# elu+1 split between VectorE and GpSimd, one task for the memory products, and another seed for the planned order

## The chip, the cores and the metric

The kernel runs on one core of a Trainium2 chip. Its metric is device time in microseconds, the median of several runs. The engines in the profile are PE (TensorE, matrix multiplications; PEld is its weight load), DVE (VectorE), ACT (ScalarE), POOL (GpSimd) and SP (SyncE, which here issues DMAs). Each engine works through its own list of instructions in order and waits on semaphores for what other engines have to deliver.

## The reference

The input `x` has 2048 tokens of 512 features in bfloat16. Two branches are mixed by a gate per token: a gated attention with a compressive memory over four segments of 512 tokens and 32 heads of width 16, and a gated feed-forward layer of width 1792.

```python
phi = lambda t: jnp.where(t > 0, t + 1.0, jnp.exp(t))
for s in range(N):                       # four segments of 512 tokens
    logits = einsum('bhqd,bhkd->bhqk', qs, ks) * scale + mask
    a_dot = einsum('bhqk,bhkd->bhqd', softmax(logits), vs)
    pq = phi(qs)
    num = einsum('bhld,bhde->bhle', pq, M)
    den = einsum('bhld,bhd->bhl', pq, z)[..., None] + 1e-06
    outs.append(g * (num / den) + (1.0 - g) * a_dot)
    pk = phi(ks)
    M = M + einsum('bhld,bhle->bhde', pk, vs)
    z = z + einsum('bhld->bhd', pk)
a = concat(outs) @ wo
b = (gelu(x @ w_gate) * (x @ w_up)) @ w_down
out = sigmoid(x . gate_w) * a + (1 - sigmoid(x . gate_w)) * b
```

## The kernel before

**Layout.** `x` is held transposed (`xT`, features on the partitions) and the weights lie in on-chip memory. Everything on PE runs in tiles of 128 partitions by 512 tokens, accumulated in PSUM, of which there are eight banks (`ps`). In the attention phase most matrix products are split into four narrow ones that run side by side (`dense`, L479); one such quad works 512 columns.

**Stages.** In the first 66 us the keys, queries and values of segment 0 and the gate projections of all segments are computed (L565, L475), and ScalarE applies gelu. Then comes the attention phase. Each segment has 20 logit slots (`logit_slot`, L735): each fills two pairs of PSUM banks, ScalarE takes the exponential into `pT` (L757, two instructions of 128x1024 a slot) and GpSimd masks the diagonal blocks (L766). After some slots come the products with the values (`pv_group`, L785), which VectorE transposes out of PSUM (L803) and normalizes (L813 to L829).

**Fillers.** Between the slots PE computes other things: the up projections (`up_group`, L479 with `wup`, taken out of PSUM by VectorE in L657), the queries, keys and values of the next segment (`qk_group`, `v_group`, taken out by L314 or L316), the update of the memory (`m_update`, L894), the memory's denominator and numerator for the present segment (`mem_den` with `zbd`, `mem_num` with `Mbd`) and the output of the previous segment (`out_group`). `NUPS` says how many up groups go with each segment.

**elu+1.** `phi` makes a map of keys or queries for two chunks of 128 features at once, a tile of 128x1024. ScalarE writes the exponential to `E` (L847); VectorE writes max(x, 0) + 1 to `Q` (L852) and then the minimum of `E` and `Q` to the map (L856), since elu+1 is min(exp(x), max(x, 0) + 1). It is run twelve times: for the keys of segments 0, 1 and 2 (two each, `phi_k`) and the queries of segments 1, 2 and 3 (two each, `phi_q`). A key map goes through two DMA transposes on the sync queue (L883) and is the stationary operand of the memory update. A query map is read by the denominator and numerator products. There is one buffer each for `E`, `Q` and `pkT`.

**Memory.** After the second update of a segment VectorE forms `Mbd` from the accumulated memory in four products (L918) on 32 partitions each, and `zbd` (L922). In the planner the four are four tasks.

**The order.** It is not written out by hand. `Sched` takes all tasks with an engine, a cost in nanoseconds, dependencies, buffers taken and freed, and a priority, and simulates the engines once, on the host. At each step the engine that can start soonest takes, among the tasks that are ready, the one of smallest priority. Logit slots are held to a pace (`due`), which spreads the remaining dense work of PE over the remaining slots. Tasks marked `port=True` are ones that the planner lets wait for a GpSimd task that is running, and the other way round. The priorities of fillers on PE get a random offset, drawn with `SEED` between -`SPREAD` and +`SPREAD`. The instructions are emitted in the resulting order, and on the chip every engine keeps to it.

Of the kernel before, what the change touches and what calls it, by code (L numbers as in the profile page):

```python
# [10 lines left out]
ALU = mybir.AluOpType  # L11
# [6 lines left out]
DH = 16  # L18
# [16 lines left out]
SLACK = 300  # L35
PORTPEN = 0
NWARM = 6
NUPS = (28, 10, 9, 9)
ATT = 5
SEED = 1  # L40
SPREAD = 1.5
SHAPES = {"gen": [(b,) for b in range(NBANK)],
          "pair": [(b, b + 1) for b in range(NBANK - 1)]}
WIDTH = {k: len(v[0]) for k, v in SHAPES.items()}
# [14 lines left out]
class Sched:  # L59
# [10 lines left out]
    def __init__(self, rings):  # L70
        self.tasks = []
        self.bufs = rings
        self.rng = Random(SEED)

    def add(self, engs, cost, fn, **kw):

        if "PE" in engs and 0 < kw["prio"] < 9000:
            kw["prio"] += self.rng.uniform(-SPREAD, SPREAD)
        engs = {engs: cost} if isinstance(engs, str) else dict(zip(engs, cost))
        t = Task(engs, fn, **kw)  # L80
        t.seq = len(self.tasks)
        self.tasks.append(t)
        return t
# [205 lines left out]
def kernel(  # L289
# [15 lines left out]
    nc = tc.nc  # L305
# [20 lines left out]
    add = S.add  # L326

    def ctile(name, shape, dtype=BF):
        return cp.tile(shape, dtype, name=name, tag=name)
# [16 lines left out]
    def rtile(ring, shape, dtype=BF, pool=None):  # L346
        pool = pool or (pools["wp"] if ring in WP else rp)
        return pool.tile(shape, dtype, name=ring, tag=ring, bufs=RINGS[ring])
# [16 lines left out]
    zbd = ctile("zbd", [P, NCH * (P + 2)])  # L365
    bdeb = ctile("bdeb", [P, NCH, 8, DH])
    Mbd = ctile("Mbd", [P, NCH, 8, DH])
    Macc = ctile("Macc", [P, NCH, 2, VW], F32)
# [71 lines left out]
    def group(name, cost, mms, prio, deps, alloc="gen", also=None, **kw):  # L440

        box = {}

        def fn(e):
            box["t"] = pair(t) if alloc == "pair" else bank(t)
            if also:
                also[1]()
            mms(box["t"])
        t = add("PE", cost, fn, prio=prio, deps=deps, alloc=[alloc] + ([also[0]] if also else []),
                **kw)  # L450
        return t, box
# [3 lines left out]
    def evac(engs, g, box, fn, prio=0.0, deps=(), alloc=(), frees=(), ring="gen", cost=None):  # L455
        engs = [engs] if isinstance(engs, str) else engs
        cost = [EV[e] if cost is None else cost for e in engs]
        return add(engs, cost, lambda e: fn(e, box["t"]), prio=prio, deps=[g] + list(deps),
                   alloc=alloc, frees=[(ring, g)] + list(frees))
# [11 lines left out]
    def dense(t, lhsT, rhs, start, stop):  # L471


        if not tiled:
            nc.tensor.matmul(t, lhsT=lhsT, rhs=rhs, start=start, stop=stop)  # L475
            return
        for j in range(4):
            a = slice(32 * j, 32 * j + 32)
            nc.tensor.matmul(t[a, :], lhsT=lhsT[:, a], rhs=rhs, start=start, stop=stop,  # L479
                             tile_position=(0, 32 * j), skip_group_check=True)  # L480
# [113 lines left out]
    TAB = {}  # L594
# [93 lines left out]
    for s in range(NSEG):  # L688
        if s == 3:
            gate_rows(-960 + 20 * s)  # L690
        for hp in range(HS // 2):
            gate_pair(s, hp, -959 + 20 * s + hp)
            if s == 1 and hp == HS // 2 - 1:
                g, box = group("bps", 60, f_bps, -922, [a_be])
# [145 lines left out]
    PQ, PKt, PHI, PKD, RMt = {}, {}, {}, {}, {}  # L840

    def phi(src, deps, prio, mk, ring):
        box = {}

        def f_e(_):
            box["E"] = rtile("E", [P, 2, L])
            nc.scalar.activation(box["E"][:, :, :], src()[:, :, :], AF.Exp)  # L847


        def f_q(_):  # L850
            box["Q"] = rtile("Q1", [P, 2, L])
            nc.vector.tensor_scalar(out=box["Q"][:, :, :], in0=src()[:, :, :], scalar1=0.0,  # L852
                                    scalar2=1.0, op0=ALU.max, op1=ALU.add)

        def f_a(_):
            nc.vector.tensor_tensor(mk()[:, :, :], box["E"][:, :, :], box["Q"][:, :, :],  # L856
                                    op=ALU.min)
        e = add("ACT", 960, f_e, prio=prio, deps=deps + [TAB["first_x"], opened], alloc=["E"])
        q = add("DVE", 325, f_q, port=True, prio=5, deps=[e], alloc=["Q1"])
        return add("DVE", 602, f_a, port=True, prio=5, deps=[q], alloc=[ring],  # L860
                   frees=[("E", e), ("Q1", q)])

    def phi_q(s, pr, prio):
# [22 lines left out]
    def m_update(s, pr, prio):  # L886

        def mms(t):
            for i in range(2):
                for kt in range(KT):  # L890
                    for j in range(4):
                        a = slice(32 * j, 32 * j + 32)
                        h = 16 * pr + 8 * i + 2 * j
                        nc.tensor.matmul(t[a, 2 * i * VW:2 * (i + 1) * VW],  # L894
                                         lhsT=PKt[(s, pr)][:, i, kt, a],
                                         rhs=vz[s % 2][:, kt, h * VW:(h + 2) * VW],
                                         start=(kt == 0), stop=(kt == KT - 1),
                                         tile_position=(0, 32 * j), skip_group_check=True)
        g, box = group("M", 8 * 28, mms, prio,
                       [PKD[(s, pr)]] + [EVV[(s, kt)] for kt in range(KT)]  # L900
                       + (TAB[("mbd", s - 1)] + [TAB[("zbd", s - 1)]] if s else []),
                       frees=[("pk", PKD[(s, pr)])])
        MUT[s].append(g)

        def f_acc(e, t):
            dst = Macc[:, 2 * pr:2 * pr + 2, :, :].rearrange("p c e w -> p (c e w)")
            if s == 0:
                nc.vector.tensor_copy(dst, t[:, 0:4 * VW])
            else:
                nc.vector.tensor_add(dst, t[:, 0:4 * VW], dst)  # L910
        acc = evac("DVE", g, box, f_acc, cost=200)
        TAB[("acc", s, pr)] = acc
        if pr == 0:
            return

        def f_mbd(j):
            a, hh = slice(32 * j, 32 * j + 32), slice(2 * j, 2 * j + 2)
            return lambda _: nc.vector.tensor_mul(Mbd[a, :, hh, :], Macc[a, :, :, 0:DH],  # L918
                                                  bdeb[a, :, hh, :])

        def f_zbd(_):
            nc.vector.tensor_mul(  # L922
                zbd[:, :].rearrange("p (c n) -> p c n", c=NCH)[:, :, 0:P]
                .rearrange("p c (j m) -> p c j m", j=4)[:, :, :, 0:2],
                Macc[:, :, :, DH][:, :, None, :].to_broadcast((P, NCH, 4, 2)),
                bd[:, :, 0].rearrange("p (j e) -> p j e", j=4)[:, None, :, :]
                .to_broadcast((P, NCH, 4, 2)))
        deps = [TAB[("acc", s, 0)], acc, t_eb] + [TAB[("num", s, c)] for c in range(NCH) if s]
        TAB[("mbd", s)] = [add("DVE", 240, f_mbd(j), port=True, prio=3, deps=deps)
                           for j in range(4)]  # L930
        TAB[("zbd", s)] = add("DVE", 125, f_zbd, port=True, prio=3, deps=deps + ([TAB[("den", s)]] if s else []))

    def mem_den(s, prio):
# [31 lines left out]
    def mem_num(s, c, prio):  # L965
        def mms(t):
            dense(t, Mbd[:, c, :, :].rearrange("p h d -> p (h d)"), PQ[(s, c // 2)][:, c % 2, :],
                  True, True)
        bx = {}
        g, box = group("num", MM, mms, prio,  # L970
                       TAB[("mbd", s - 1)] + [TAB[("den", s)], PHI[("q", s, c // 2)]],
                       also=("Tm", lambda: bx.update(T=rtile("Tm", [P, QB, 2, DH], F32))),
                       frees=[("pq", PHI[("q", s, c // 2)])])
        TAB[("num", s, c)] = g

        def f_T(_, t):
            nc.vector.transpose(bx["T"][:, :, :, :].rearrange("p a e d -> p (a e d)"), t[:, :])

        def f_n(_):
            NMt[(s, c)] = rtile("Nm", [P, QB, 2, DH])  # L980
            nc.vector.tensor_mul(NMt[(s, c)][:, :, :, :], bx["T"][:, :, :, :],
                                 RMt[s][:, :, 2 * c:2 * c + 2][:, :, :, None]
                                 .to_broadcast((P, QB, 2, DH)))
        ev = evac("DVE", g, box, f_T)
        NMT[("Nm", (s, c))] = add("DVE", 593, f_n, port=True, prio=2.5, deps=[ev, TAB[("rm", s)]],
                                  alloc=["Nm"], frees=[("Tm", g), ("rm", TAB[("rma", s)])])
# [40 lines left out]
    ups = [(s, hs) for s in range(NSEG) for hs in range(HS)]  # L1027
    UPS = [[ups.pop(0) for _ in range(n)] for n in NUPS]

# [29 lines left out]
    for s in range(NSEG):  # L1059
        for t in range(NSLOT):  # L1060
# [6 lines left out]
            c, w = divmod(t, 5)  # L1067
# [37 lines left out]
```

## Time and profile before

| | us |
|---|---|
| median of three runs | 275.12 (274.56 to 275.5) |
| profiled execution, its own time | 274.56 |
| its span | 272.7 |
| ScalarE exponentials of logits (L757), 160 of mean 1031 ns | 153.7 busy |
| up groups taken out of PSUM (L657), 56 of mean 680 ns | 37.8 busy |
| value products taken out of PSUM (L803), 32 of mean 708 ns | 22.7 busy |
| exponentials of elu+1 (L847), 12 | 12.9 busy |

The span runs from the first to the last instruction in the profile; the time of a run also has what lies around it. A row of a group gives busy time, mean duration, and the idle time of the engine just before the group's instructions with what ended it. In the rows of a timeline the first number is the start, the second the duration. A row of waits gives the sum, the number and the longest of them.

### The profile page before, as it was taken

The page shows a single profiled execution, that of the slowest core. Times are in us where ns is not written, and L with a number is a line of the kernel's source. Part 1 is how long each engine was busy: PE and PEld are TensorE (multiplying, and loading weights), DVE is VectorE, ACT ScalarE, POOL GpSimd, SP SyncE. Part 2 cuts the span into 40 slices and gives each one's busy share as a digit, 9 for nine tenths or more (in the row PEclk, how much of TensorE's full clock was granted, in tenths as well). Part 3 has the DMA queues.
Part 4 walks back from the last instruction along what each step waited for, and adds up shares of the span by engine and source line. Part 5 has one row for each costly group of instructions (what it writes and reads, how often), then busy time and mean ns, then how long its engine had stood idle before and what let it go on. Part 6 is the DMA issues. An engine that isn't in the chain of part 4 may idle for free.

```text
span 272.7 us, 10273 instructions
## 1 busy us (share of the span) xinstructions
PE 266.6 (98%) x4569; PEld 127.0 (47%) x4575; DVE 171.5 (63%) x323; ACT 211.6 (78%) x234; POOL 106.2 (39%) x209
## 2 busy tenths in 40 slices
PE   7999999999999999999999999999999999999995
PEld 4444444444444554454444454444444444444454
DVE  3340003000888898989998989999858698765140
ACT  3445555646987799998978998899998999889812
POOL 8100000070343444355444545455555456664500
PEclk9999999999999999999999999999999999999999
DMA  7994790000023000220001121000000000000002
GB/s 210 369 135 97 256 352 10 0 0 2 5 45 38 2 2 2 41 43 2 2 23 22 42 41 41 5 2 2 22 22 4 22 24 2 22 22 22 22 5 78
DMA packets 22244, 14.02 MB, mean 51 GB/s; under 512 B 14136, under 2 KB 21176, under 8 KB 22200
## 3 DMA queue, kind: packets, MB, share of 16 engines
q1 hardware_dynamic: 21624, 12.85, 17.9%
q8 instruction: 35, 0.57, 0.9%
q10 hardware_dynamic: 576, 0.52, 0.6%
q14 instruction: 9, 0.07, 0.1%
HBM read 8.13 MB, written 2.10 MB: 37 GB/s over the span
## 4 chain that ended last, share of the span: by engine, by line
PE 97%; ACT 1%; issue 1%; DVE 0%; ACTq 0%
PE ps L479 57%; PE ps L475 20%; PE ps L735 10%; PE ps L785 6%; PE ps L565 1%; PE ps L529 1%; ACT pT L757 1%; PE ps L894 1%; PE ps L550 0%; PE ps L601 0%; DVE xT L316 0%; ACT osb L1017 0%; DVE wdn L392 0%; PE ps L666 0%; ACTq L1017 0%
## 5 line engine op out<-in xcount | busy, mean ns | idle before, releaser
L757 ACT ACTIVATE pT<-ps 128x1024 bf16<-128x1024 f32 x160 | 153.7, 1031 | 15.9 <-PE ps L735 14.7
L766 POOL TENSOR_SCALAR_AFFINE_SELECT pT<-pT 128x512 bf16<-128x512 bf16 (+1 forms) x160 | 94.3, 592 | 104.0 <-ACT pT L757 103.2
L479 PE MATMUL ps<-wdn,G 128*32 128x512 bf16 (+1 forms) x952 | 59.1, 368 | 0.2 <-ACT pT L757 0.2
L479 PE MATMUL ps<-xT,wup 128*32 128x512 bf16 x896 | 55.5, 380 | 0.0
L657 DVE TENSOR_TENSOR G<-ps,G 128x512 bf16<-128x512 f32 x56 | 37.8, 680 | 18.3 <-PE ps L479 18.0
L475 PE MATMUL ps<-xT,wga 128*128 128x512 bf16 x219 | 48.4, 379 | 0.4 <-issue 0.2
L647 ACT ACTIVATE G<-ps 128x1024 bf16<-128x1024 f32 x28 | 28.7, 1024 | 23.5 <-PE ps L475 22.8
L475 PEld LDWEIGHTS <-wga 128*128 128x128 bf16 x224 | 21.7, 98 | 26.4 <-issue 0.4
L803 DVE STREAM_TRANSPOSE T<-ps 128x512 f32<-128x512 f32 x32 | 22.7, 708 | 17.7 <-PE ps L785 11.6
L479 PEld LDWEIGHTS <-wup 128*32 128x32 bf16 x896 | 23.2, 96 | 21.1 <-issue 2.1
L479 PEld LDWEIGHTS <-G 128*32 128x32 bf16 x952 | 22.4, 96 | 19.4 <-issue 4.2
L618 POOL COPY G_87<-tt 32x16 f32<-32x16 f32 x16 | 3.1, 195 | 47.8 <-DVE tt L610 47.2
L735 PE MATMUL ps<-qT,kT 16*128 16x256 bf16 (+2 forms) x320 | 17.4, 274 | 0.0
L735 PE MATMUL ps<-qT,kO 32*128 32x128 bf16 (+2 forms) x320 | 17.3, 272 | 0.0
L479 PE MATMUL ps<-wo,xT 128*32 128x512 bf16 (+1 forms) x272 | 16.5, 367 | 0.0
L479 PEld LDWEIGHTS <-xT 128*32 128x32 bf16 x464 | 11.5, 96 | 10.3 <-issue 2.1
L735 PEld LDWEIGHTS <-kT 16*128 16x128 bf16 x320 | 6.8, 92 | 18.9 <-issue 18.8
L735 PEld LDWEIGHTS <-kO 32*128 32x128 bf16 x320 | 6.9, 92 | 12.1 <-issue 12.0
L479 PE MATMUL ps<-xT,wq 128*32 128x512 bf16 x192 | 12.5, 380 | 0.0
L479 PE MATMUL ps<-xT,wk 128*32 128x512 bf16 x192 | 12.5, 380 | 0.0
L1017 ACT ACTIVATE osb<-ps,omz 128x512 bf16<-128x512 f32 (+1 forms) x8 | 5.1, 635 | 9.4 <-PE ps L479 9.4
L479 PE MATMUL ps<-wv,xT 128*32 128x512 bf16 x192 | 12.4, 381 | 0.0
(116 smaller groups left out, 249.6 us busy)
## 6 DMA issues: line engine op xcount, KB each, us to landing
out_dram<-osb SPq DMA_DIRECT2D x15, 128.0 KB, 1.8
wup<-in_B_w_up_dram SPq DMA_DIRECT2D x1, 1792.0 KB, 8.2
wdn<-in_B_w_down_dram SPq DMA_DIRECT2D x1, 1792.0 KB, 13.7
wga<-in_B_w_gate_dram SPq DMA_DIRECT2D x1, 1280.0 KB, 10.2
wq<-in_A_wq_dram SPq DMA_DIRECT2D x1, 512.0 KB, 4.8
wga<-in_B_w_gate_dram SPq DMA_DIRECT2D x1, 512.0 KB
wv<-in_A_wv_dram SPq DMA_DIRECT2D x1, 512.0 KB, 7.3
wo<-in_A_wo_dram SPq DMA_DIRECT2D x1, 512.0 KB, 9.3
```

Of the source, the lines that this page charges most:

```text
L475: nc.tensor.matmul(t, lhsT=lhsT, rhs=rhs, start=start, stop=stop)
L479: nc.tensor.matmul(t[a, :], lhsT=lhsT[:, a], rhs=rhs, start=start, stop=stop, tile_position=(0, 32 * j), skip_group_check=True)
L529: nc.tensor.matmul(pair(w)[:, 0, :], lhsT=warm[:, 0:P], rhs=warm, start=True, stop=True)
L618: nc.gpsimd.tensor_copy(G2[dst, s, :], z[src, :, 0])
L647: ge = evac("ACT", g, box, lambda e, t: nc.scalar.activation(dst, t[:, :, :], AF.Gelu_apprx_tanh), cost=920, ring="pair")
L657: UPT[(s, hs)] = evac("DVE", g, box, lambda e, t: nc.vector.tensor_mul(G[:, s, hs, :], t[:, :], G[:, s, hs, :]))
L735: nc.tensor.matmul(A[j // 2][:, j % 2, at * P:(at + nq) * P], lhsT=l, rhs=r, start=True, stop=True, tile_position=(32 * j, 0))
L757: nc.scalar.activation(pT[(s, t, h)][:, :, :], A[h][:, :, :], AF.Exp, scale=0.25)
L766: nc.gpsimd.affine_select(out=v, in_=v, pattern=pat, compare_op=ALU.is_ge, fill=0.0, base=0, channel_multiplier=-1)
L785: nc.tensor.matmul(t[32 * j:32 * j + 32, qb * P:(qb + nq) * P], lhsT=vz[s % 2][:, kt, h * VW:h * VW + 32], rhs=pT[(s, t0 + w, j // 2)][:, ...
L803: nc.vector.transpose(TT[key][:, e, :, :].rearrange("p a b -> p (a b)"), t[:, :])
L1017: nc.scalar.activation(bx["o"][:, cols], bank(first)[:, cols], AF.Copy, scale=f)
```

## The change

Three things are edited.

1. In `phi`, VectorE computes max(x, 0) into `Q` and clips `E` at 1 in place, two tasks; GpSimd adds the two into the map, a third task with a planner's cost of 2090 ns. The value is the same, exp(min(x, 0)) + max(x, 0). Before, VectorE did it alone in two tasks.
2. The four products that form `Mbd` become one task of four instructions with a cost of 1000 ns, where they were four tasks of 240 ns. What depended on the four depends on the one.
3. `NUPS`, `SEED` and `SPREAD` have other values. The sum of `NUPS` is 56 as before.

As the planner works on all of it, the order on every engine may differ throughout the attention phase.

```diff
-NUPS = (28, 10, 9, 9)
+NUPS = (26, 12, 10, 8)
 ATT = 5
-SEED = 1
-SPREAD = 1.5
+SEED = 6
+SPREAD = 3.0
...
         def f_q(_):
             box["Q"] = rtile("Q1", [P, 2, L])
-            nc.vector.tensor_scalar(out=box["Q"][:, :, :], in0=src()[:, :, :], scalar1=0.0,
-                                    scalar2=1.0, op0=ALU.max, op1=ALU.add)
+            nc.vector.tensor_scalar_max(box["Q"][:, :, :], src()[:, :, :], 0.0)
+
+        def f_m(_):
+            nc.vector.tensor_scalar_min(box["E"][:, :, :], box["E"][:, :, :], 1.0)
 
         def f_a(_):
-            nc.vector.tensor_tensor(mk()[:, :, :], box["E"][:, :, :], box["Q"][:, :, :],
-                                    op=ALU.min)
+            d = mk()
+            nc.gpsimd.tensor_add(d[:, :, :], box["E"][:, :, :], box["Q"][:, :, :])
         e = add("ACT", 960, f_e, prio=prio, deps=deps + [TAB["first_x"], opened], alloc=["E"])
         q = add("DVE", 325, f_q, port=True, prio=5, deps=[e], alloc=["Q1"])
-        return add("DVE", 602, f_a, port=True, prio=5, deps=[q], alloc=[ring],
+        m = add("DVE", 330, f_m, port=True, prio=5, deps=[e])
+        return add("POOL", 2090, f_a, prio=5, deps=[m, q], alloc=[ring],
                    frees=[("E", e), ("Q1", q)])
...
-        def f_mbd(j):
-            a, hh = slice(32 * j, 32 * j + 32), slice(2 * j, 2 * j + 2)
-            return lambda _: nc.vector.tensor_mul(Mbd[a, :, hh, :], Macc[a, :, :, 0:DH],
-                                                  bdeb[a, :, hh, :])
+        def f_mbd(_):
+            for j in range(4):
+                a, hh = slice(32 * j, 32 * j + 32), slice(2 * j, 2 * j + 2)
+                nc.vector.tensor_mul(Mbd[a, :, hh, :], Macc[a, :, :, 0:DH], bdeb[a, :, hh, :])
...
-        TAB[("mbd", s)] = [add("DVE", 240, f_mbd(j), port=True, prio=3, deps=deps)
-                           for j in range(4)]
+        TAB[("mbd", s)] = add("DVE", 1000, f_mbd, port=True, prio=3, deps=deps)
```

More of the change, by code (lines that the diff above doesn't have):

```diff
@@ L900, in m_update @@
                        [PKD[(s, pr)]] + [EVV[(s, kt)] for kt in range(KT)]
-                       + (TAB[("mbd", s - 1)] + [TAB[("zbd", s - 1)]] if s else []),
+                       + ([TAB[("mbd", s - 1)], TAB[("zbd", s - 1)]] if s else []),
                        frees=[("pk", PKD[(s, pr)])])
@@ L970, in mem_num @@
         g, box = group("num", MM, mms, prio,
-                       TAB[("mbd", s - 1)] + [TAB[("den", s)], PHI[("q", s, c // 2)]],
+                       [TAB[("mbd", s - 1)], TAB[("den", s)], PHI[("q", s, c // 2)]],
                        also=("Tm", lambda: bx.update(T=rtile("Tm", [P, QB, 2, DH], F32))),
```

## The prediction

> **What bounds the kernel now.** I read the page's header and busy row first, then who PE (TensorE) waited for, then the busy time of the engines by stretch, and last the instructions that the change touches.
>
> ```profile
> span 272.7 us, 10273 instructions
> PE 266.6 (98%) x4569; PEld 127.0 (47%) x4575; DVE 171.5 (63%) x323; ACT 211.6 (78%) x234; POOL 106.2 (39%) x209
> ...
> PE 97%; ACT 1%; issue 1%; DVE 0%; ACTq 0%
> ```
>
> The chain that ended last is PE for 97% of the span. PE is idle for 272.7 - 266.6 = 6.1 us in all. The waits of PE over the whole span, and below them the busy time of each engine (columns PE, PEld, DVE, ACT, POOL) in the attention phase and in its densest part:
>
> ```profile
> PE ps L529 <- DVE wdn L392: 1.3, 1, 1.3
> PE ps L479 <- ACT pT L757: 0.7, 2, 0.5
> PE ps L565 <- DVE xT L316: 0.6, 1, 0.6
> ...
> 66.00:260.00 194.00, 193.26 (x4021) 91.41 (x4024) 157.76 (x286) 173.61 (x191) 94.27 (x160) 1.00 0.09 19
> 100.00:190.00 90.00, 90.00 (x1896) 42.30 (x1892) 82.89 (x157) 82.51 (x93) 44.29 (x74) 1.00 0.10 20
> ```
>
> The reader is to see three things. From 66 to 260 us PE misses 0.74 us (the two waits of 0.7 us on L757; the rest of its idle time is start and drain, which the change leaves alone). Between 100 and 190 us VectorE has only 7.1 us idle and ScalarE 7.5 us. GpSimd has room, 45.7 of 90 us. The granted clock is 1.00 throughout, so the clock moves nothing here.
>
> The instructions in question, first by group, then three of them in order of time:
>
> ```profile
> L766 POOL TENSOR_SCALAR_AFFINE_SELECT pT<-pT 128x512 bf16<-128x512 bf16 x96 | 68.2, 714 | 56.3 <-ACT pT L757 55.6
> L766 POOL TENSOR_SCALAR_AFFINE_SELECT pT<-pT 128x256 bf16<-128x256 bf16 x64 | 26.2, 409 | 47.7 <-ACT pT L757 47.6
> ...
> 102.46 0.42 DVE L852 TENSOR_SCALAR Q_1498<-qT 128x1024 bf16<-128x1024 bf16 x1
> 102.98 1.05 DVE L856 TENSOR_TENSOR pq<-E,Q_1498 128x1024 bf16<-128x1024 bf16 x1
> ...
> 102.85 0.64 POOL L766 TENSOR_SCALAR_AFFINE_SELECT pT<-pT 128x512 bf16<-128x512 bf16 x1 [0.28 <-ACT pT L757]
> ```
>
> The last three lines show what VectorE and GpSimd do to each other. The minimum of L856 takes 0.65 to 0.70 us in ten of its twelve places. Beside a select that ran from 102.85 to 103.49 it took 1.05 us, so it ended 0.54 us after the select: it lost about the time for which the select was still running.
>
> **The change part by part.** *VectorE's share of elu+1.* Twelve maps are built (keys of segments 0 to 2, queries of 1 to 3, two each). Gone are twelve maximum-plus-one of mean 412 ns (L852) and twelve minima of mean 732 ns (L856): 13.7 us. Added are twelve maxima and twelve clips at 1 of the same tile (128x1024 bf16, one tensor and constants), the form of L852: 24 x 412 ns = 9.9 us. VectorE saves 3.8 us, none of it on PE's path by itself.
>
> *GpSimd's new add.* No row shows a two-input operation on GpSimd. An undisturbed select costs 0.41 us for 256 elements a partition and 0.64 us for 512, so 0.90 us per 1000; carried on to 1024 elements that is 1.10 us with one input. Twice that, 2.20 us, is the upper bound for two. The planner's 2090 ns lies near the upper end, and its select costs are 0.05 us below the undisturbed rows (365 and 590 against 410 and 640 ns), so I take 2.2 us. Twelve adds are 26 us; GpSimd goes from 94 to some 121 of the 194 us of the attention phase. It does not become the bound. [...]
>
> *VectorE held up by the add.* While a select runs, VectorE instructions with two SBUF inputs or of the constant form (L493, L816, L821, L826, L852, L856, L951, L957, L981) are stretched as above. I placed an add of 2.2 us behind each of the twelve maps in the old order (0.4 us after L856 began, or when the select then running ended) and read off when the next such instruction started. The rest of the add that it would have to sit out is 1.44, 0.47, 0.48, 0, 0.37, 1.97, 1.06, 0.05, 0.44, 0.02, 1.13 and 0 us, in sum 7.4 us. Behind the held instruction stand the PSUM evacuations on VectorE's queue (L657, L316, L803), for which PE's next groups wait. Cover: one dense group keeps PE busy for some 0.88 us (four quads of 0.22 us in the order of time). What exceeds that in the four large waits is 0.56 + 1.09 + 0.18 + 0.25 = 2.1 us. This is the term I put on the path. Its lower bound is 0 (the order is planned anew with the add in it; VectorE's demand from 100 to 190 us is 82.9 - 3.0 + 5.5 = 85.4 of 90 us and still fits). Its upper bound is the case in which each add holds VectorE for all of its 2.2 us, priced among the rivals. Halfway between would be 5 us; I stay at 2.1 because the individual waits, not their worst case, are what the rows give.
>
> *Late selects.* A select that comes up while an add runs starts up to 2.2 us later. The value matmuls (L785) wait for it: 18 of the 32 groups start 0.15 to 0.32 us after their last select. With that little slack a late select would stop PE at once if the order were the old one; the order is planned with the add's cost, so the new plan puts other groups in front. The probabilities' buffers give cover: the tightest exponential starts 2.8 us after the group that frees its buffer, so ScalarE isn't stopped by one add. On the path I take 0. Without that cover: in the old order ten of the twelve adds have a select within their first 1.5 us, which would start 0.7 to 2.2 us late, 17 us in sum; two of five slots end a group's selects, so some 0.4 x 17 = 7 us would reach PE.
>
> *Late maps.* From the exponential's end the map is now ready after a clip of 0.41 us, a wait for a select (0 to 1.9 us) and 2.2 us, against 0.7 us: 2 to 4 us later. Behind it on the sync queue stand the two transposes of the key map and the output stores; neither is waited for at once: the last key map's transposes were issued by 161.7 us and its matmuls (L894) ran at 182.5 us. The denominator matmuls (L479 with zbd) are tighter, 0.6 us after the map in segment 1 and 1.6 us in segment 3. They can be put behind other dense groups; in segment 3, where PE's only two waits lie (0.51 us at 224.3 and 0.23 us at 234.8), few are left. The single E buffer is held for about 4.4 us instead of 2.6, while the first two exponentials stand 2.9 us apart, so the second moves by 1.5 us. I take 0 for these, with 1 us at the upper end.
>
> *One task for the four products of L918.* The same instructions, four of about 0.28 us. In two of the three places something of 0.74 to 0.78 us slipped in between; it now waits up to 0.8 us. That is below the cover of 0.88 us: 0, at most 1.6 us.
>
> *Other counts per segment, seed and spread.* The 56 up groups stay 56, every matmul stays, so PE's busy time stays. At best the two waits vanish (-0.7 us); at worst some more such waits appear, and three of 0.5 us would be +1.5 us. I take 0.
>
> Sum: 2.1 us. The profiled execution took 274.56 us with a span of 272.7, so 1.86 us lie around the span. Span after: 274.8 us; time 276.7 us by that execution. The median of the three runs, 275.12, is 0.56 us above it, which makes **277.2 us**.
>
> **The rivals.** *No change, 275.1 us.* The new plan hides every held instruction, as VectorE's demand still fits (85.4 of 90 us) and PE's work is the same. For it: PE waits almost nowhere today although selects and maps already disturb each other. Against: from 100 to 190 us three engines are above 91%, and the rows above hold waits longer than one group. This is the case on the other side, not slower; it decides if no wait exceeds the 0.88 us cover.
>
> *Faster, 274.4 us.* The two waits in segment 3 vanish and nothing new appears. PE's 0.74 us from 66 to 260 us is all there is to win, because the work of PE, the start and the drain are the same; more than 0.8 us is hardly possible.
>
> *The lock sets the pace, 285 us.* Each add holds VectorE for its full 2.2 us. Nine of the twelve fall into 100 to 190 us: 19.8 - 3.0 saved = 16.8 us more demand against 7.1 us idle leaves 9.7 us, and 275.1 + 9.7 = 284.8. For it: 68 of VectorE's 156 instructions in that stretch are of the held forms (L918 and L922 among them). Against: read one by one, the old order gives 5.5 us in that stretch, not 19.8.
>
> **How the numbers follow.** Forecast (276 to 281 us): 0.52. No change: 0.22. Faster: 0.06. Lock (above 281 us): 0.20. A measurement of this kernel can tell about 0.3%, 0.8 us, from no change; so faster 0.06, same 0.22, slower 0.72. Some 1 in 10 lies below 274.6 (the faster case and the lower edge of no change), and half of the lock case above 283: the range is 274.6 to 283 us. The forecast's own range is 276 to 281.
>
> **What would show it.** The add on GpSimd lasts 2.0 to 2.4 us undisturbed; maximum and clip about 0.41 us each; VectorE's busy time is up by 2 to 6 us in all (-3.8 saved, +7.4 held); PE's busy time stays within 1 us of 266.6 and its idle time from 66 to 260 us rises from 0.7 to 2 to 4 us, put down to VectorE evacuations or late selects. It would be wrong if the add took 1.1 us, if held VectorE instructions aren't stretched by it, or if PE's idle time stayed below 1.5 us. An idle time of over 6 us would speak for the lock.

## The result, and the profile after

| | before | after |
|---|---|---|
| median (us) | 274.87 (4 runs, 274.56 to 275.5) | 276.8 (4 runs, 276.5 to 277.01) |
| ratio | | 1.0067, 95% interval 1.0044 to 1.0089 |
| profiled execution (us) | 274.56 | 276.84 |
| its span (us) | 272.7 | 275.1 |
| first logit matmul to last matmul of PE (us) | 203.44 | 205.46 |

The changed kernel is slower by 0.67%. The last row leaves the start out, which differs by some tenths of a us between executions; it is read off the order of time and used below to compare orders.

The page's header and its chain by engine, after:

```profile
span 275.1 us, 10302 instructions
PE 267.2 (97%) x4569; PEld 126.4 (46%) x4575; DVE 173.5 (63%) x323; ACT 211.9 (77%) x234; POOL 128.8 (47%) x221
...
PE 89%; DVE 4%; DMA 3%; issue 1%; ACT 1%; ACTq 0%
```

PE's busy time moved by 0.6 us, VectorE's by 2.0, GpSimd's by 22.6. VectorE, at 0% of the chain before, is now 4% of it. The waits of PE, and the same two stretches as before (columns PE, PEld, DVE, ACT, POOL):

```profile
PE ps L479 <- DVE G L657: 1.6, 1, 1.6
...
PE ps L565 <- DVE xT L316: 0.6, 1, 0.6
```

```profile
66.00:260.00 194.00, 191.99 (x3971) 90.11 (x3972) 159.71 (x286) 173.35 (x191) 115.91 (x171) 1.00 0.08 19
100.00:190.00 90.00, 89.27 (x1848) 42.26 (x1851) 78.29 (x146) 80.53 (x92) 55.19 (x78) 1.00 0.09 20
```

From 66 to 260 us PE now misses 2.0 us instead of 0.74, and nearly all of it is one wait of 1.57 us behind a VectorE evacuation. The stretch around it, VectorE and GpSimd first, then PE:

```profile
95.73 3.23 DVE L921 TENSOR_TENSOR Mbd<-Macc,bdeb 32x128 bf16<-32x128 f32 x4
95.81 2.18 POOL L858 TENSOR_TENSOR pq<-E,Q_1238 128x1024 bf16<-128x1024 bf16 x1
...
98.99 1.29 DVE L657 TENSOR_TENSOR G<-ps,G 128x512 bf16<-128x512 f32 x2
...
100.33 1.91 PE L479 MATMUL ps<-wv,xT 128*32 128x512 bf16 x32 [1.57 <-DVE G L657]
```

The durations of the twelve products, shortest, median and longest in ns:

```profile
L921 DVE TENSOR_TENSOR Mbd<-Macc,bdeb x12: 271/286/2120, 95.7 to 198.2; 32x128 bf16<-32x128 f32 x12
```

Read the order of time from the bottom. PE waits for a PSUM bank that the evacuations at 98.99 give back. They stand behind the four products of `Mbd` (L921). The four take 3.23 us instead of the 1.1 us of four undisturbed ones. The first began just before GpSimd's add (95.81 to 97.99) and took 0.27 us; the second began at 96.02, beside the add, and took 2.12 us, so that it ended 0.14 us after the add; the other two, in the same task, came after it. What the add does to VectorE elsewhere shows in the groups, three of them before and then the same three after; mean of one before and after: L821 720 and 893 ns, L493 418 and 514, the `Mbd` products (L918 before, L921 after) 338 and 481:

```profile
L821 DVE TENSOR_TENSOR N<-T,r 128x512 bf16<-128x512 f32 x16 | 11.5, 720 | 0.3
L493 DVE TENSOR_SCALAR kO<-kT,odd 128x512 bf16<-128x512 bf16 x16 | 6.4, 418 | 1.5 <-ACT kT L314 1.5
L918 DVE TENSOR_TENSOR Mbd<-Macc,bdeb 32x128 bf16<-32x128 f32 x12 | 4.1, 338 | 0.2
```

```profile
L821 DVE TENSOR_TENSOR N<-T,r 128x512 bf16<-128x512 f32 x16 | 14.3, 893 | 0.3
L493 DVE TENSOR_SCALAR kO<-kT,odd 128x512 bf16<-128x512 bf16 x16 | 7.9, 514 | 0.5 <-ACT kT L314 0.5
L921 DVE TENSOR_TENSOR Mbd<-Macc,bdeb 32x128 bf16<-32x128 f32 x12 | 5.8, 481 | 0.1
```

Nearly all of this growth is four instructions. Of the twelve adds only four have a VectorE instruction of such a form begin beside them: the product above (2.12 us), one of L493 (2.18 us) and two of L821 (1.99 and 2.37 us). Against their usual times they lose 6.6 us together, and PE waits visibly behind the first one alone.

### The profile page after: what moved, and what is told of

Same layout as the page of the kernel before. It is cut to its first block, busy times and chain, and to the rows that moved or that the text cites. A ratio compares the mean times of both kernels' runs of the same rounds, so it can differ in the third digit from the quotient of the medians.

```text
span 275.1 us, 10302 instructions
## 1 busy us (share of the span) xinstructions
PE 267.2 (97%) x4569; PEld 126.4 (46%) x4575; DVE 173.5 (63%) x323; ACT 211.9 (77%) x234; POOL 128.8 (47%) x221
## 4 chain that ended last, share of the span: by engine, by line
PE 89%; DVE 4%; DMA 3%; issue 1%; ACT 1%; ACTq 0%
PE ps L479 53%; PE ps L475 20%; PE ps L735 9%; PE ps L785 6%; DMA wq<-in_A_wq_dram 2%; DMA wdn<-in_A_x_dram 1%; DVE G L657 1%; ACT pT L757 1%; DVE Mbd L921 1%; DVE vz_82 L316 0%; DVE kT L316 0%; PE ps L896 0%; PE ps L601 0%; DVE E L854 0%; DVE xT L829 0%
## 5 line engine op out<-in xcount | busy, mean ns | idle before, releaser
L766 POOL TENSOR_SCALAR_AFFINE_SELECT pT<-pT 128x512 bf16<-128x512 bf16 (+1 forms) x160 | 91.5, 579 | 80.5 <-ACT pT L757 80.2
L657 DVE TENSOR_TENSOR G<-ps,G 128x512 bf16<-128x512 f32 x56 | 37.9, 681 | 21.4 <-PE ps L479 21.4
L803 DVE STREAM_TRANSPOSE T<-ps 128x512 f32<-128x512 f32 x32 | 22.7, 710 | 18.6 <-PE ps L785 15.1
L479 PEld LDWEIGHTS <-wup 128*32 128x32 bf16 x896 | 22.4, 96 | 22.3 <-issue 4.0
L479 PEld LDWEIGHTS <-G 128*32 128x32 bf16 x952 | 23.0, 97 | 19.0 <-issue 2.7
L735 PE MATMUL ps<-qT,kO 32*128 32x128 bf16 (+2 forms) x320 | 18.0, 272 | 0.2 <-ACT pT L757 0.2
L735 PE MATMUL ps<-qT,kT 16*128 16x256 bf16 (+2 forms) x320 | 17.6, 274 | 0.0
L735 PEld LDWEIGHTS <-kT 16*128 16x128 bf16 x320 | 6.9, 92 | 19.6 <-issue 19.5
L821 DVE TENSOR_TENSOR N<-T,r 128x512 bf16<-128x512 f32 x16 | 14.3, 893 | 0.3
L735 PEld LDWEIGHTS <-kO 32*128 32x128 bf16 x320 | 7.1, 92 | 12.2 <-issue 12.1
L1018 ACT ACTIVATE osb<-ps,omz 128x512 bf16<-128x512 f32 (+1 forms) x9 | 5.8, 641 | 8.8 <-PE ps L479 8.8
```

The source lines that it names most:

```text
L657: UPT[(s, hs)] = evac("DVE", g, box, lambda e, t: nc.vector.tensor_mul(G[:, s, hs, :], t[:, :], G[:, s, hs, :]))
L735: nc.tensor.matmul(A[j // 2][:, j % 2, at * P:(at + nq) * P], lhsT=l, rhs=r, start=True, stop=True, tile_position=(32 * j, 0))
L766: nc.gpsimd.affine_select(out=v, in_=v, pattern=pat, compare_op=ALU.is_ge, fill=0.0, base=0, channel_multiplier=-1)
L803: nc.vector.transpose(TT[key][:, e, :, :].rearrange("p a b -> p (a b)"), t[:, :])
L821: nc.vector.tensor_mul(NN[key][:, :, :, :].rearrange("p a e d -> p e a d"), TT[key][:, :, :, 0:DH], RR[key][:, :, :, :].to_broadcast((P, 2 ...
L1018: nc.scalar.activation(bx["o"][:, cols], bank(first)[:, cols], AF.Copy, scale=f)
```

## The experiments

Three explanations stood against each other: the add holds VectorE up (A), the other order costs the time whatever the form of elu+1 (B), and late selects stop PE (C). The unchanged kernel was measured beside each of three groups of experiments, with medians of 274.9, 274.7 and 274.6 us; ratios are to it. Rows and stretches of PE come from one profiled execution of each kernel.

### One part of the change alone

`params_only`:

```diff
-NUPS = (28, 10, 9, 9)
+NUPS = (26, 12, 10, 8)
-SEED = 1
-SPREAD = 1.5
+SEED = 6
+SPREAD = 3.0
```

> The kernel before with only the other counts per segment, seed and spread. Theory A (the GpSimd add holds VectorE and that makes the 2 us): 274.9 us within 0.8, PE idle from 66 to 260 us about 0.7 us. Rival B (the other seed's order is simply the worse one): 276.2 to 277.2 us. Rival C (late selects): as A.

Measured 277.3 us, ratio 1.0089 (1.0068 to 1.0111). There is no add in this kernel and GpSimd is busy 105.8 us as before. Rival B holds here, 0.1 us above its range: the other seed, spread and counts cost 2.4 us by themselves. The waits of PE in the attention phase are small and scattered, the largest of them behind evacuations on VectorE:

```profile
PE ps L479 <- DVE Tm L977: 0.6, 1, 0.6
PE ps L785 <- DVE G L657: 0.5, 1, 0.5
PE ps L479 <- DVE T L803: 0.4, 1, 0.4
```

`mbd_only`: the kernel before with the products' tasks of the change.

```diff
...
-        TAB[("mbd", s)] = [add("DVE", 240, f_mbd(j), port=True, prio=3, deps=deps)
-                           for j in range(4)]
+        TAB[("mbd", s)] = add("DVE", 1000, f_mbd, port=True, prio=3, deps=deps)
```

> The kernel before with only the four Mbd products as one task. Theory A: 274.9 us within 0.8, since without an add on GpSimd the block lasts some 1.1 us. Rival B: within 1 us of before in either direction, as any new order is. A reading above 276.2 us would say that the block alone is what costs.

Measured 276.17 us, ratio 1.0043 (1.0015 to 1.0071). This lies above what either theory expected (at most 275.7 and 275.9 us) and just below the 276.2 us that would have put it on the block. The blocks last 1.3 to 1.5 us, and PE's largest wait is 0.68 us on ScalarE in segment 3, far from any `Mbd` product. That speaks for the new order and against the block as what costs here, though no run separates the two.

`phi_only`: the kernel before with the `phi` of the change (its diff is that part of the diff above).

> The kernel before with only elu+1 on VectorE and GpSimd, order planned anew with the seed of before. Theory A: 275.8 to 278 us, with a wait of PE above 1 us behind a VectorE evacuation that stood behind a held instruction. Rival B: 274.9 us within 0.8. Rival C: 275.8 to 278 us too, but with PE waiting for value matmuls (L785) whose selects were late.

Measured 277.54 us, ratio 1.0095 (1.0072 to 1.0118). The time is as A and C expected, but PE's longest wait, 0.62 us at 228.4 us, stands behind value-product evacuations (L803) that no add had held; no wait of 1 us is there, and none on a select. Its adds held eleven VectorE instructions for 11.8 us in all, more than in the changed kernel, and still no large wait followed. The reason given for A is not shown by this run.

### The add without a plan for it

`old_order_add` keeps the old order and puts the add where the minimum stood.

```diff
         def f_a(_):
-            nc.vector.tensor_tensor(mk()[:, :, :], box["E"][:, :, :], box["Q"][:, :, :],
-                                    op=ALU.min)
+            nc.vector.tensor_scalar_min(box["E"][:, :, :], box["E"][:, :, :], 1.0)
+            nc.gpsimd.tensor_add(mk()[:, :, :], box["E"][:, :, :], box["Q"][:, :, :])
```

> The old order kept as it was planned, with the minimum of L856 replaced by the clip on VectorE and the add on GpSimd at the same place: the add is unplanned. This measures the terms of the prediction in the order in which they were read: held instructions alone (Theory A) give 277.0 us, with VectorE's busy time up by 3 to 6 us. Rival C: late selects reach PE as well, by the working up to 7 us, so 279 to 284 us, with PE's idle time in front of L785. Rival B: 275 to 276 us.

Measured 288.04 us, ratio 1.049 (1.0457 to 1.0523), 4 us beyond C's upper end. The waits of PE:

```profile
PE ps L785 <- POOL pT L766: 6.7, 13, 0.8
PE ps L479 <- DVE G L657: 1.4, 1, 1.4
...
PE ps L479 <- POOL pq L856: 0.8, 1, 0.8
```

These are the prediction's terms one by one. Late selects: 6.7 us in 13 visible waits of the value matmuls; the working for an order without cover said some 7. VectorE held up: eight instructions lost 8.3 us beside adds, where the working had 7.4, and one wait of 1.44 us stands behind evacuations (the row has 1.4), after L816 had taken 1.96 us beside an add; the working said 2.1 for PE. A late map: one wait of 0.84 us at the denominator; 1 us was the upper end. PE's idle time in the attention phase is 9.97 us (0.74 before), so 9.2 us of the 12.6 us by which the stretch from the first logit matmul to the last matmul grew (215.99 against 203.44) show as waits. Much of the rest lies with the value matmuls as well: by the distances between successive starts they come 9.4 us later in sum, 2.7 us more than their visible waits. The plan is thus worth some 10 us to the add form: `phi_only`, with the same form and settings planned anew, took 277.54 us, and PE waits there for no select at all.

### The changed kernel's own order

`after_mbd_late` moves one task in the finished order.

```diff
     S.plan()
+    for s in (0,):
+        o, m = S.order, TAB[("mbd", s)]
+        i = o.index(m)
+        j = [k for k in range(i + 1, len(o)) if o[k].eng == "DVE"][1]
+        o.insert(j, o.pop(i))
     S.emit()
```

> The changed kernel in its own order, with one thing moved: the block of four Mbd products of segment 0 stands two VectorE instructions later, behind the two evacuations (L657) that it held up. Theory A (the one wait of 1.57 us at 100.3 us comes from the products sitting out the add, and it stays lost): 275.2 us within 0.6, and no wait above 0.5 us near 100 us. Rival B (that wait is made up for by slack later, or another one takes its place): 276.5 to 277 us as the changed kernel.

Measured 276.21 us, ratio 1.0067 (1.0051 to 1.0084). The wait of 1.57 us is gone, and two others stand near it:

```profile
PE ps L479 <- DVE vz L316: 0.6, 1, 0.6
PE ps L479 <- DVE T L803: 0.4, 1, 0.4
```

They are 0.40 us at 99.6 and 0.65 us at 101.7, together 1.05. The products, now at 97.26, no longer run 3.23 but 1.58 us; VectorE's queue is still late behind them. The stretch of PE is 205.06 us against 205.46: 0.4 us came back, of 1.57. The ratio is the changed kernel's, 1.0067; only the spans are a little shorter, 274.2 to 274.7 us in six executions against 274.8 to 275.1 in four. Neither expectation is met fully: the wait is mostly displaced.

`after_add_dve` leaves the order and issues the add on VectorE.

```diff
-            nc.gpsimd.tensor_add(d[:, :, :], box["E"][:, :, :], box["Q"][:, :, :])
+            nc.vector.tensor_add(d[:, :, :], box["E"][:, :, :], box["Q"][:, :, :])
```

> The changed kernel in its own order, with the add issued on VectorE instead of GpSimd at the same place. GpSimd holds nobody any longer; VectorE gets twelve adds of some 0.69 us more. Theory A: 274.8 to 275.8 us, the wait at 100.3 us gone or below 0.5 us. Rival B (the order, not the add, costs the time): 276.3 to 277.3 us, spread over waits elsewhere.

Measured 275.79 us, ratio 1.004 (1.0027 to 1.0054), at the upper edge of A's range. The wait at 100.3 is gone (0.17 us are left at 98.8):

```profile
95.59 1.27 DVE L921 TENSOR_TENSOR Mbd<-Macc,bdeb 32x128 bf16<-32x128 f32 x4
96.89 0.69 DVE L858 TENSOR_TENSOR pq<-E,Q 128x1024 bf16<-128x1024 bf16 x1
97.50 1.28 DVE L657 TENSOR_TENSOR G<-ps,G 128x512 bf16<-128x512 f32 x2
```

The four products take 1.27 us, the add 0.69 us on VectorE, and the evacuations start 1.5 us earlier than in the changed kernel. PE's idle time from 66 to 260 us is 0.77 us, as in the kernel before. The stretch of PE is 204.52 us: 0.94 us less than in the changed kernel, 1.08 more than before. So in this order the place of the add costs 0.9 us, although VectorE does twelve instructions more without it. The ratios alone would leave this open, as their intervals overlap (1.0027 to 1.0054, and 1.0044 to 1.0089 for the changed kernel); the spans of the executions do not: 273.6 to 274.3 us in five, against 274.8 to 275.1 us in four. The other 1.1 us are what is left over, and by this subtraction they go with the order. They show as no single wait. PE's logit groups (L735), busy time and mean of one, are in the changed kernel

```profile
L735 PE MATMUL ps<-qT,kO 32*128 32x128 bf16 (+2 forms) x320 | 18.0, 272 | 0.2 <-ACT pT L757 0.2
L735 PE MATMUL ps<-qT,kT 16*128 16x256 bf16 (+2 forms) x320 | 17.6, 274 | 0.0
```

and before

```profile
L735 PE MATMUL ps<-qT,kO 32*128 32x128 bf16 (+2 forms) x320 | 17.3, 272 | 0.0
L735 PE MATMUL ps<-qT,kT 16*128 16x256 bf16 (+2 forms) x320 | 17.4, 274 | 0.0
```

with the same means: the starts of matmuls within a slot lie further apart, by 0.9 us in sum over the 80 slots (35.6 against 34.7 us of busy time). The same groups come to 35.6 us in `after_add_dve` and 35.7 us in `params_only`. The mean logit matmul is recorded with 0.27 us, while the starts within a slot lie 15 to 17 ns apart in the mean; a wait that is shorter than a recorded time leaves no idle time, so the busy share of PE doesn't show these. What makes them, and why other groups gain and lose about as much as each other in the new order, stays open.

`after_min` undoes `phi` and keeps the rest, planned anew (diff as above, reversed).

> The changed kernel with elu+1 as the minimum on VectorE again, order planned anew; the one task for the products and the other seed stay. Theory A: 275 to 275.8 us. Rival B: 276 to 277.5 us, as the kernel before with the other seed alone (277.3) has shown that the seed costs as much without any add.

Measured 275.66 us, ratio 1.0036 (1.0024 to 1.0049): inside A's range, and 0.3% below the changed kernel, with intervals that touch; the spans, 273.6 to 274.0 us against 274.8 to 275.1, lie clearly apart. PE waits nowhere above 0.26 us in the attention phase; the stretch is 204.38 us.

`after_mbd_four` undoes the one task and keeps the rest, planned anew.

> The changed kernel with the four Mbd products as four tasks again, order planned anew. Theory A: 275.2 to 276.2 us, because an evacuation can slip between the products. Rival B (each new order costs something of its own): anywhere from 275.5 to 278 us.

Measured 282.58 us, ratio 1.0289 (1.026 to 1.0318): far outside what either theory had for it, and the reverse of what A expected of undoing the block. PE's rows in segment 3, and the granted clock (the column behind the counts; 0.50 is half speed) in short stretches:

```profile
226.32 0.28 PE L735 MATMUL ps<-qT,kT 16*128 16x256 bf16 x2 [0.89 <-ACT pT L757]
...
227.23 0.39 PE L735 MATMUL ps<-qT,kO 32*128 32x512 bf16 x3 [0.41 <-ACT pT L757]
228.15 0.28 PE L735 MATMUL ps<-qT,kO 32*128 32x256 bf16 x2 [0.52 <-ACT pT L757]
229.06 0.61 PE L735 MATMUL ps<-qT,kO 32*128 32x256 bf16 x10 [0.63 <-ACT pT L757]
229.98 1.90 PE L479 MATMUL ps<-pq,zbd 128*32 128x512 bf16 x16 [0.31 <-ACT pT L757]
```

```profile
225.00:227.00 2.00, 0.93 (x21) 0.21 (x10) 1.76 (x5) 2.00 (x3) 0.63 (x1) 1.00 0.20 66
227.00:229.00 2.00, 0.68 (x5) 0.19 (x5) 1.93 (x4) 2.00 (x4) 1.75 (x2) 0.85 0.00 0
229.00:231.00 2.00, 1.63 (x22) 0.92 (x25) 1.97 (x2) 2.00 (x4) 2.00 (x2) 0.50 0.00 0
231.00:233.00 2.00, 2.00 (x23) 0.47 (x12) 1.40 (x3) 1.68 (x2) 2.00 (x5) 0.50 0.00 0
...
235.00:237.00 2.00, 2.00 (x56) 1.12 (x52) 0.89 (x2) 0.69 (x2) 0.41 (x1) 0.94 0.00 0
```

The order has logit slots back to back with nothing between them. Each then goes at the pace of ScalarE's exponentials, ScalarE is busy throughout, and PE idles 2.8 us between 225.4 and 230. Then the clock drops to 0.50 for about 6.8 us. PE idles for 0.9 us of these; half of the other 5.9 us, some 2.9 us, is an estimate of what is lost. The Trainium skill, TensorE: Matmul & The Clock Gate, section "Part 1: The HAM clock gate", has the clock fall to half after an idle window of some 3.4 us. Here no single idle piece is above 0.89 us; the lowered clock came in a stretch in which PE was busy for 1.6 of 4 us (225 to 229). The measurement decides: many short waits were enough.

`four_last_dve` asks whether the late map is the cause. It is `after_mbd_four` in the same order with one add on VectorE.

```diff
-    def phi(src, deps, prio, mk, ring):
+    def phi(src, deps, prio, mk, ring, on=nc.gpsimd):
...
-            nc.gpsimd.tensor_add(d[:, :, :], box["E"][:, :, :], box["Q"][:, :, :])
+            on.tensor_add(d[:, :, :], box["E"][:, :, :], box["Q"][:, :, :])
...
-                                [EVQK[("q", s, 2 * pr)], EVQK[("q", s, 2 * pr + 1)]], prio, mk, "pq")
+                                [EVQK[("q", s, 2 * pr)], EVQK[("q", s, 2 * pr + 1)]], prio, mk, "pq",
+                                on=nc.vector if (s, pr) == (3, 1) else nc.gpsimd)
```

> The kernel of after_mbd_four in the same order, with the add of one map only, the second query map of segment 3, on VectorE instead of GpSimd. Theory D (the late map makes the denominator matmuls late, PE idles for some 3 us near 228 us, and the lowered clock that follows, 0.50 for about 8 us, costs 4 us more): 275.5 to 278 us, granted clock 1.00 from 220 to 250 us. Rival (PE idles there because the order has nothing else to offer, add or no add): 281 us or more, clock still lowered.

Measured 282.12 us, ratio 1.0266 (1.023 to 1.0302). Theory D falls. The last map's add now ran on VectorE, from 228.53 to 229.64 us, where it had ended at 230.40 on GpSimd, and the denominator still began at 230.16, with the clock at 0.50 after it:

```profile
230.16 1.51 PE L479 MATMUL ps<-pq,zbd 128*32 128x512 bf16 x16 [0.52 <-ACT pT L757]
```

```profile
231.00:234.00 3.00, 3.00 (x32) 0.94 (x28) 2.05 (x4) 2.70 (x4) 1.68 (x3) 0.50 0.00 0
```

In `after_mbd_four`, too, the denominator had begun before the add of that map ended, at 229.98. What stands in front of it on PE is the run of logits, which waits for ScalarE. That the map is planned late may be why the planner had nothing else to put there; this was not tried.

### The form of elu+1 at other orders

`phi_mbd` is the changed kernel with the counts, seed and spread of before.

> The kernel before with elu+1 on two engines and the one task for the products, with the counts, seed and spread of before. Pair of mbd_only (276.17). Theory A (the add costs about 2 us whatever the order): 277.5 to 279 us. Rival B (orders scatter by as much as the form costs): anywhere from 275.5 to 283 us.

Measured 277.96 us, ratio 1.0119 (1.0091 to 1.0148), 1.8 us above `mbd_only`. That is within A's range, but B's range holds it too.

`min_seed2` and `add_seed2` are the kernel before and `phi_only` with another seed.

```diff
-SEED = 1
+SEED = 2
```

> The kernel before with seed 2. Theory A: within 1 us of 275. Rival B (the order of seed 1 is a good draw, others are worse without any add): 276 to 279 us.

> The kernel before with elu+1 on two engines and seed 2, pair of min_seed2. Theory A: 1.5 to 3 us above min_seed2. Rival B: the difference lies between -2 and +6 us, with the sign not told beforehand; above 4 us only if the clock is lowered somewhere after a wait of 2 us or more.

Measured 282.77 us, ratio 1.0288 (1.0261 to 1.0315), for the minimum and 278.87 us, ratio 1.0146 (1.0122 to 1.0171), for the add. All expectations were missed: the minimum lies above both of its ranges, and the add is 3.9 us faster than the minimum, where A had it 1.5 to 3 us slower and B at most 2 us faster. The minimum's order has the same defect as `after_mbd_four`, at its end:

```profile
258.00:262.00 4.00, 2.43 (x34) 0.83 (x37) 1.80 (x3) 4.00 (x6) 2.89 (x5) 0.83 0.00 0
262.00:266.00 4.00, 3.92 (x46) 1.75 (x48) 0.72 (x1) 2.56 (x3) 1.85 (x4) 0.50 0.00 0
```

Logit slots back to back from 256 us on, ScalarE busy for all of 258 to 262 us, and half the clock for 6.8 us, from 260.7 to 267.5. No add is in this kernel. With that the two forms can be compared at five settings:

| order planned with | minimum, ratio to before | add, ratio to before |
|---|---|---|
| settings of before | 1 | 1.0095 |
| and products as one task | 1.0043 | 1.0119 |
| other counts, seed, spread | 1.0089 | 1.0289 |
| the same, products as one task | 1.0036 | 1.0067 (the change) |
| settings of before, seed 2 | 1.0288 | 1.0146 |

The add form is slower in four of five pairs, by 0.3 to 2.0%, and faster by 1.4% in the fifth. The two largest differences, 2.0 and 1.4%, each have on one side an order in which the clock fell (`after_mbd_four` and `min_seed2`); the other three are 0.3 to 1.0%. Within a column the orders differ by 2.2 to 2.9%. No version ran faster than the kernel before.

## Why the prediction was right, point by point

The forecast was 277.2 us and the measurement 276.8; the mechanism forecast, a VectorE instruction held by the add with evacuations behind it, is the one large wait in the changed kernel's trace. But the sum came out right with two terms off in opposite directions: 2.1 us for held instructions and nothing for the order stood against 0.9 and 1.1 us. That the total fits within 0.4 us is in part luck.

*The add's duration.* 2.2 us were taken; ten of twelve lasted 2.12 to 2.20 us, the others 2.26 and 2.56, above what was called the upper bound. Right.

*VectorE's share.* Saved 3.8 us, measured 3.6 (13.7 against 4.8 + 5.4 us). Held 7.4 us; the groups L821, L493, `Mbd` and L816 grew by 2.8 + 1.5 + 1.7 + 0.5 = 6.5 us, while the products of L981 (L982 after) lost 0.6; four instructions held beside adds make up 6.6 us. VectorE's busy time rose by 2.0 us, at the lower edge of the 2 to 6 forecast. Right.

*What of it reaches PE.* This was 2.1 us. In the changed order one wait of 1.57 us shows it, and taking the add from GpSimd gave 0.9 us back. Right in kind, too large by about a factor of two: in this order only four of the twelve adds held an instruction, and only one of the four had evacuations behind it that PE was about to need.

*The one task for the products.* This was put at 0, because a delay of 0.8 us is below the cover of 0.88 us. That step failed. The list of forms that an add holds up was written without L918, which is counted only in the rival of the lock, so the delay was priced without an add: beside one, a single product took 2.12 us and the block 3.23 us. The wait needs the add, as it is gone in `after_add_dve`, and without an add the block of `mbd_only` lasts 1.3 to 1.5 us. That it needs the block as well is not shown: the four tasks were not run in this order.

*Late selects and late maps.* 0, with the old order's numbers as the price without cover. Right for the changed kernel, where PE waits for no select. In the old order with the add the map's 0.84 us fits, and the selects cost 6.7 us in visible waits, but 9.4 us by the distances of the starts, more than the 7 worked out.

*Other counts, seed and spread.* 0, at most 1.5 us. This was mis-sized: alone they cost 2.4 us, and of the change's 2.0 us in PE's stretch 1.1 remain when the add is taken off GpSimd. The argument that PE's work stays the same was true and not enough. The order of before is the best of those run, and another one lost 1 to 8 us with the same or nearly the same work (`mbd_only`, `params_only`, `min_seed2`).

*The rivals.* The rival of no change is refuted by the ratio's interval, 1.0044 to 1.0089. The lock at 285 us did not come in the planned order, yet an unplanned add gave 288 us, more than half of its visible waits through selects and not through VectorE.

What stays open: the form's cost over all orders, as five pairs do not agree on its sign; the part of each order's loss that no visible wait carries; and whether the 1.1 us are the order's alone, as that is a subtraction from one profiled execution of each kernel.

## What to carry to other kernels

Where one engine is busy for 97% of the span in an order found by a planner, ask of any edit first what it does to the order: here new orders alone cost 0.9 to 2.9% (`params_only`, `min_seed2`), as much as the edit in question and more. Compare forms at several seeds before giving one of them the credit. When an instruction is fused into a block, price it beside its worst neighbour, here an add on GpSimd, not its usual one.

## What the runs showed of the hardware

- A two-input add of 128x1024 bf16 on GpSimd takes 2.13 us, on VectorE 0.69 us.
- VectorE instructions of certain forms that begin while it runs end only after it, however small they are: products of two operands in SBUF, the on-chip memory outside PSUM (L816, L821, L826, `Mbd` and others), and a tile with a constant (L493). In eight profiles 51 such instructions began beside an add, and none ended before it. A product of 32x128 elements took 2.12 us instead of 0.28, one of 128x32 elements 1.96 us instead of 0.19, L493 2.18 us instead of 0.35. In the changed kernel they ended 0.14 to 0.55 us after the add.
- Evacuations from PSUM are not held: 19 began beside an add in the changed kernel, and none took more than 3% over its usual time (L657 0.69 us).
- PE's granted clock fell to 0.50 in three profiles (`after_mbd_four`, `four_last_dve`, `min_seed2`). In the emptiest 4 us of each, before or around the fall, PE was busy for 1.55, 1.54 and 1.79 us, and idle for no more than 0.9 us at once. The clock stayed low for 6.8, 3.4 and 6.8 us, until 4 to 6 us after the last wait of PE there. In the changed kernel PE was busy for 2.43 of 4 us (96.33 to 100.33) with one idle piece of 1.57 us, and the clock stayed at 1.00. So in these runs the busy share of some 4 us told the cases apart, and the longest idle piece did not.
- In `after_mbd_four` the lowered clock is, by the estimate above, 2.9 us of the 7.8 us by which PE's stretch exceeds that of before (211.24 against 203.44).
